# Loading attention and MoE operands as fp16 through GpSimd's software DMA queue, with VectorE pairing the heads

## Chip, cores and metric

The kernel runs on one core of one Trainium2 chip. The metric is the time of one execution in microseconds (us); several runs are made, and their median is compared. The engines are named as the profile names them: PE is TensorE's matmul, PEld its weight load, DVE is VectorE, ACT is ScalarE, POOL is GpSimd, and SP is the engine that issued every transfer so far. SPq and POOLq are their instruction queues.

## Reference, cut to what matters

An attention with an extra one in its denominator feeds a feed-forward layer that takes the largest of three products. The shapes are 8 batches, 12 heads, 448 positions and 64 values for each head, so 3584 tokens of 768 values; all four weights are 768 x 768. Every input and the output are fp32.

```python
scores = (q @ k.T) / sqrt(64)
m = max(scores, axis=-1)
e = exp(scores - m)
attn = e / (sum(e) + exp(-m) + 1e-09)
a = attn @ v                                  # [8, 12, 448, 64]
x = a.transpose(0, 2, 1, 3).reshape(3584, 768)
h = maximum(maximum(x @ w1, x @ w2), x @ w3)
out = h @ w_out
```

## Kernel before

**Tiles.** The work on q, k and v is cut into 24 groups: batch b and a third g of the heads, so four heads (GH) in each group. The 448 positions lie on 112 partitions with 4 positions (NCH) each. The function load_group (L78) brings q, k and v of one group as fp32 into tiles ld_q, ld_k and ld_v of [112, 4 heads, 4, 64], with three buffers for each name. One such transfer moves 448 runs of 1 KB, one for each partition and head. load_weight (L113) brings a weight in three parts of [128, 2, 768] fp32 into staging tiles wst, of which there are three buffers for all.

**Casts.** All operands of TensorE are fp16. POOL makes them. cast_qk (L133) writes q16 and k16 for each pair of heads, in the order [position, head, value] that the transposes want, in four instructions of 512 elements on each partition. cast_v (L148) multiplies v by LAMBDA = 256 in one instruction of 1024 elements. cast_weight (L124) copies each third of a weight from wst into w_sb.

**A group's work.** transpose_pair (L155) transposes k16 and q16 of a pair on PE into a PSUM tile trT (8 instructions, L161), and DVE copies that into qkT (L166). scores_visit (L169) makes two positions' worth of scores of a pair on PE (L178), and ACT takes the exponential into eT (L187). av_group (L196) makes the denominator with a matrix of ones and then the two halves of the numerator (L207); ACT makes the reciprocal as Exp(-Ln(den + 1)) in two steps (L218, L220), and DVE multiplies it in, into xT (L223). The factor 256 in v keeps the fp16 values large; it is divided out of the output at L265.

**The feed-forward pieces.** up_piece (L231) is six matmuls into one PSUM bank p_i (L237) and a DVE instruction that copies it (L245) or takes the maximum (L247). out_piece (L252) is six matmuls (L258), a DVE scaling (L265), and after every second one the stores from SP (L281). Pieces wait in a list, and moe (L298) takes them out by a credit of PE columns, so that each visit of the attention is followed by about as much feed-forward work. The PSUM pool ps1 has four banks, for trT, the three products of av_group, p_i and op_ps together.

**Order.** The schedule is written by hand: each engine runs its instructions in the order in which the program emits them, and waits where a tile isn't there. Before the loop, groups 0, 1 and 2 are requested, and groups 0 and 1 are cast. Iteration i of the loop (L324) first emits loads and casts for later groups, then four visits of group i. Visit 0 is followed by av_group of group i - 1, visits 1 and 2 by the two transpose_pair of group i + 1. The first pieces enter the list in iteration 3. The order of the loads on SP is q and k of group 0, q and k of group 1, v of both, group 2, w1, q and k of group 3, w2 of the reference's names, v of group 3, w3, group 4, w_out, group 5, and then one group in each iteration. (In the program's counting from 0 these weights are 0, 1, 2 and 3.) The stores of L281 are issued on SP too, so loads behind them wait for them.

Of the kernel before, what the change touches and what calls it, by code (L numbers as in the profile page):

```python
# [21 lines left out]
def kernel(  # L22
# [11 lines left out]
    nc = tc.nc  # L34

    B, H, S, D = q.shape
    NTOK, DM = out.shape
    DFF = moe_w1.shape[1]
    SC = 112
    NCH = S // SC  # L40
    NDC = DM // 128
    NFC = DFF // 128
    GH = 4
    NG = H // GH
    scale = 1.0 / math.sqrt(D)
# [5 lines left out]
            name=nc.get_next_instruction_name(),  # L51
# [4 lines left out]
    )  # L56

    cpool = ctx.enter_context(tc.tile_pool(name="const", bufs=1))
    ld_pool = ctx.enter_context(tc.tile_pool(name="ld", bufs=3))
    p16_pool = ctx.enter_context(tc.tile_pool(name="p16", bufs=4))  # L60
    v16_pool = ctx.enter_context(tc.tile_pool(name="v16", bufs=5))
    att_pool = ctx.enter_context(tc.tile_pool(name="att", bufs=4))
    wst_pool = ctx.enter_context(tc.tile_pool(name="wst", bufs=3))
    e_pool = ctx.enter_context(tc.tile_pool(name="e", bufs=2))
    small = ctx.enter_context(tc.tile_pool(name="small", bufs=2))
    xt_pool = ctx.enter_context(tc.tile_pool(name="xt", bufs=2))
# [9 lines left out]
    raw = {}  # L76

    def load_group(i, which="qkv", step=GH):  # L78
        b, g = groups[i]
        tiles = raw.setdefault(i, {})  # L80
        for name in which:
            tiles[name] = ld_pool.tile(
                [SC, GH, NCH, D], FP32, tag="ld_" + name, name="ld_" + name
            )
        for h0 in range(0, GH, step):
            for name in which:
                src = {"q": q, "k": k, "v": v}[name][b].rearrange(
                    "(g h) (p c) d -> g p h (c d)", g=NG, c=NCH
                )[g]
                nc.sync.dma_start(  # L90
                    out=tiles[name][:, h0 : h0 + step].rearrange("p h c d -> p h (c d)"),
                    in_=src[:, h0 : h0 + step],
                )

    load_group(0, "qk", 2)
    load_group(1, "qk")
    load_group(0, "v")
    load_group(1, "v")
    load_group(2)

    ident16 = cpool.tile([128, 128], MMDT, name="ident16")
    make_identity(nc, ident16)
    ones16 = cpool.tile([SC, 32], MMDT, name="ones16")
    nc.vector.memset(ones16, 1.0)
    one_b = cpool.tile([128, 1], FP32, name="one_b")
    nc.vector.memset(one_b, 1.0)

    w_sb = [cpool.tile([128, NDC, DFF], MMDT, name=f"w{i}") for i in range(4)]
    wout_sb = w_sb[3]

    wst_of = {}

    def load_weight(i):  # L113
        w = (moe_w1, moe_w2, moe_w3, moe_w_out)[i]
        for g in range(NG):
            wst = wst_pool.tile([128, 2, DFF], FP32, tag="wst", name="wst")
            wst_of[i, g] = wst
            if i < 3:
                src = w.rearrange("(g p hf) f -> g p hf f", g=NG, hf=2)[g]
            else:  # L120
                src = w.rearrange("(g hf p) f -> g p hf f", g=NG, hf=2)[g]
            nc.sync.dma_start(out=wst, in_=src)  # L122

    def cast_weight(i):  # L124
        for g in range(NG):
            nc.gpsimd.tensor_copy(  # L126
                out=w_sb[i][:, 2 * g : 2 * g + 2, :], in_=wst_of.pop((i, g))
            )


    state = {}

    def cast_qk(i):  # L133
        qf, kf = raw[i].pop("q"), raw[i].pop("k")
        qk16 = []
        for pr in range(GH // 2):
            q16 = p16_pool.tile([SC, NCH, 2, D], MMDT, tag=f"q16_{pr}", name=f"q16_{pr}")
            k16 = p16_pool.tile([SC, NCH, 2, D], MMDT, tag=f"k16_{pr}", name=f"k16_{pr}")
            nc.gpsimd.tensor_copy(  # L139
                out=q16, in_=qf[:, 2 * pr : 2 * pr + 2].rearrange("p h c d -> p c h d")  # L140
            )
            nc.gpsimd.tensor_copy(  # L142
                out=k16, in_=kf[:, 2 * pr : 2 * pr + 2].rearrange("p h c d -> p c h d")
            )
            qk16.append((q16, k16))
        state[i] = {"qk16": qk16, "qkT": []}

    def cast_v(i):  # L148
        v16 = v16_pool.tile([SC, GH, NCH, D], MMDT, tag="v16", name="v16")
        nc.gpsimd.tensor_scalar(  # L150
            out=v16, in0=raw[i].pop("v"), scalar1=LAMBDA, scalar2=None, op0=ALU.mult
        )
        state[i]["v16"] = v16

    def transpose_pair(i, pr):  # L155
        st = state[i]
# [39 lines left out]
    def av_group(i):  # L196
        b, g = groups[i]
        st = state.pop(i)
        eT, v16 = st["eT"], st["v16"]
        if g == 0:  # L200
            xT[b] = xt_pool.tile([128, NDC, S], MMDT, tag="xT", name="xT")

        def col_tiled(weights):
            bank = ps1.tile([128, 512], FP32, tag="bank1", name="av")
            for c in range(NCH):
                for hh in range(GH):
                    nc.tensor.matmul(  # L207
                        out=bank[32 * hh : 32 * hh + 32, 0:S],
                        lhsT=weights(hh, c),
                        rhs=eT[:, hh, c, :],  # L210
                        start=(c == 0),
                        stop=(c == NCH - 1),
                    )
# [6 lines left out]
        nc.scalar.activation(out=rb, in_=lnd, func=AF.Exp, scale=-1.0)  # L220
        for hf in range(2):
            num = col_tiled(lambda hh, c: v16[:, hh, c, hf::2])
            nc.vector.tensor_tensor(  # L223
                out=xT[b][:, 2 * g + hf, :], in0=num[:, 0:S], in1=rb, op=ALU.mult
            )
# [88 lines left out]
    visits = [(pr, cs) for pr in range(2) for cs in ((0, 1), (2, 3))]  # L314
    NI = len(groups)

    cast_qk(0)
    cast_qk(1)
    cast_v(0)
    cast_v(1)  # L320
    transpose_pair(0, 0)
    transpose_pair(0, 1)

    for i in range(NI):  # L324
        b, g = groups[i]
        if i == 0:
            cast_qk(2)
            cast_v(2)
            load_weight(0)
            cast_weight(0)  # L330
            load_group(3, "qk")
            cast_qk(3)
        elif i == 1:
            load_weight(1)
            cast_weight(1)
            load_group(3, "v")
            cast_v(3)
        elif i == 2:
            load_weight(2)
            cast_weight(2)  # L340
            load_group(4)
            cast_qk(4)
            cast_v(4)
            load_weight(3)
            cast_weight(3)
            load_group(5)
            cast_qk(5)
            cast_v(5)
        elif i + 3 < NI:
            load_group(i + 3)  # L350
            cast_qk(i + 3)
            cast_v(i + 3)
        for vi, (pr, cs) in enumerate(visits):
            scores_visit(i, pr, cs)
            if vi == 0:
                spare = gap - av_cols
                moe(spare / 2)
                if i > 0:
                    av_group(i - 1)
                moe(spare / 2)  # L360
                if i > 0 and g == 0:
                    add_pieces(b - 1)
            elif vi < 3:
                moe((gap - tr_cols) / 2)
# [38 lines left out]
```

## Time and profile before

| what | value |
|---|---|
| median of three runs (lowest, highest) | 393.98 us (389.93, 394.03) |
| the profiled execution's own time | 395.06 us |
| its span in the trace | 393.3 us |
| bytes read from HBM / written | 42.47 MB / 11.01 MB |
| POOL instructions | 138, busy 139.8 us |
| q, k, v transfers of 448 KB | 24 + 23 + 23, and 4 halves of 224 KB for group 0 |
| weight transfers of 768 KB | 9 + 3 |

A page of the profile has the engines' busy time, then the span in 40 slices (each digit is a busy share in tenths), the DMA queues, the chain of work that ended last, and the costliest groups of instructions. A row of a group gives line, engine, operation, out<-in with shapes and count, then total busy us and mean ns of one, then the idle time of the engine ahead of it and what ended it. The chain is followed back from the end: each step is what released the next one. Rows of the view by windows give, for a stretch of time, the busy us of each engine (with the number of its instructions), the clock granted to PE as a share of full speed, the mean busy share of the 16 DMA engines (it can exceed 1, since packets overlap) and GB/s. Rows of the timeline give start, length, engine, line and tiles.

### The profile page before, as it was taken

The numbers are of one execution on the slowest core, as the hardware profiler recorded it, in microseconds if no ns is written. First come the engines' busy times: TensorE is split into PE (matmuls) and PEld (weight loads), VectorE is DVE, ScalarE is ACT, GpSimd is POOL, SyncE is SP. The second block draws the span as 40 slices with busy tenths as digits, with TensorE's granted clock in tenths as the row PEclk, the third lists the DMA queues.
The fourth block names the chain that finished last, engine by engine and source line by source line (L and its number), as shares of the span: only waits on it lengthen the run. The fifth ranks groups of instructions, "written<-read, shape, count | busy, mean of one in ns | idle before, by whom it ended". The sixth has DMA issues, their size and how long they took to land.

```text
span 393.3 us, 7451 instructions
## 1 busy us (share of the span) xinstructions
PE 365.3 (93%) x3120; PEld 174.0 (44%) x3120; DVE 173.9 (44%) x298; ACT 192.8 (49%) x241; POOL 139.8 (36%) x138
## 2 busy tenths in 40 slices
PE   2886739999999999999999999999999999999995
PEld 1232314444444544445444544444444554445552
DVE  1122213543543644544544544544544554544553
ACT  1876405556555555555455564566364465462000
POOL 3876766990492007700572027500580000000000
PEclk9997758999999999999999999999999999999999
DMA  8999999954980289305980299205960320004005
GB/s 194 225 311 311 303 286 240 236 123 119 240 185 2 53 204 260 68 0 147 226 171 2 66 242 231 47 1 164 244 135 2 83 82 0 2 2 120 2 0 161
DMA packets 40067, 53.96 MB, mean 137 GB/s; under 512 B 2273, under 2 KB 34529, under 8 KB 40033
## 3 DMA queue, kind: packets, MB, share of 16 engines
q1 hardware_dynamic: 40032, 53.49, 56.5%
q8 instruction: 24, 0.39, 0.4%
q14 instruction: 11, 0.08, 0.1%
HBM read 42.47 MB, written 11.01 MB: 136 GB/s over the span
## 4 chain that ended last, share of the span: by engine, by line
PE 85%; DMA 9%; SPq 3%; POOL 1%; issue 0%; DVE 0%; POOLq 0%
PE p_i L237 43%; PE op_ps L258 14%; PE av L207 13%; PE stp L178 10%; DMA wst<-in_moe_w_dram 7%; PE trT L161 4%; DMA ld_k<-in_k_dram 3%; SPq L90 3%; SPq L122 1%; POOL w_127 L126 0%; POOL w_126 L126 0%; POOL k_0_400 L142 0%; DVE o_sb L265 0%; POOLq L142 0%
## 5 line engine op out<-in xcount | busy, mean ns | idle before, releaser
L187 ACT ACTIVATE eT<-stp 112x896 f16<-112x896 f32 x192 | 164.8, 915 | 161.7 <-PE stp L178 161.7
L247 DVE TENSOR_TENSOR hT<-hT,p_i 128x448 f16<-128x448 f16 x96 | 59.5, 620 | 57.8 <-PE p_i L237 57.8
L237 PE MATMUL p_i<-xT,w_126 128*128 128x448 f16 x288 | 65.0, 362 | 0.1
L237 PE MATMUL p_i<-xT,w_127 128*128 128x448 f16 x288 | 62.4, 353 | 0.0
L237 PE MATMUL p_i<-xT,w_128 128*128 128x448 f16 x288 | 62.2, 353 | 0.0
L178 PE MATMUL stp<-qkT 64*128 64x448 f16 x384 | 58.2, 375 | 4.2 <-ACT eT L187 3.9
L258 PE MATMUL op_ps<-w_129,hT 128*128 128x384 f16 x336 | 59.5, 326 | 0.0
L223 DVE TENSOR_TENSOR xT<-av,rb 128x448 f16<-128x448 f32 x48 | 27.9, 620 | 69.8 <-ACT rb L220 57.7
L265 DVE TENSOR_SCALAR o_sb<-op_ps 128x384 f32<-128x384 f32 x56 | 31.2, 557 | 28.9 <-PE op_ps L258 27.8
L245 DVE CAST hT<-p_i 128x448 f16<-128x448 f32 x48 | 29.9, 624 | 30.7 <-PE p_i L237 30.7
L258 PEld LDWEIGHTS <-hT 128*128 128x128 f16 x336 | 30.9, 98 | 24.8 <-issue 6.3
L166 DVE COPY qkT<-trT 128x896 f16<-128x896 f16 x48 | 29.6, 617 | 27.2 <-PE trT L161 27.2
L237 PEld LDWEIGHTS <-w_126 128*128 128x128 f16 x288 | 26.6, 100 | 29.2 <-issue 9.2
L237 PEld LDWEIGHTS <-w_127 128*128 128x128 f16 x288 | 25.9, 98 | 29.2 <-issue 8.9
L237 PEld LDWEIGHTS <-w_128 128*128 128x128 f16 x288 | 26.0, 98 | 28.7 <-issue 7.8
L178 PEld LDWEIGHTS <-qkT 64*128 64x128 f16 x384 | 12.0, 95 | 41.4 <-issue 41.1
L207 PE MATMUL av<-eT,ones_122 112*32 112x448 f16 x384 | 24.1, 373 | 0.0
L218 ACT ACTIVATE lnd<-av,one_b 128x448 f32<-128x448 f32 x24 | 15.3, 639 | 3.7 <-PE av L207 3.7
L220 ACT ACTIVATE rb<-lnd 128x448 f32<-128x448 f32 x24 | 13.8, 577 | 0.8
L207 PEld LDWEIGHTS <-ones_122 112*32 112x32 f16 x384 | 8.3, 98 | 13.2 <-issue 9.6
L139 POOL CAST q_0_1734<-ld_q 112x512 f16<-112x512 f32 x1 | 0.6, 609 | 25.0 <-PE trT L161 25.0
L139 POOL CAST q_0_2331<-ld_q 112x512 f16<-112x512 f32 x1 | 0.6, 610 | 24.7 <-DMA ld_q<-in_q_dram 24.7
(371 smaller groups left out, 273.3 us busy)
## 6 DMA issues: line engine op xcount, KB each, us to landing
ld_v<-in_v_dram SPq DMA_DIRECT2D x24, 448.0 KB, 11.7
ld_q<-in_q_dram SPq DMA_DIRECT2D x23, 448.0 KB, 9.7
ld_k<-in_k_dram SPq DMA_DIRECT2D x23, 448.0 KB, 11.3
wst<-in_moe_w_dram SPq DMA_DIRECT2D x9, 768.0 KB, 9.3
out_dram<-o_sb SPq DMA_DIRECT2D x8, 336.0 KB, 2.8
wst<-in_moe_w_out_dram SPq DMA_DIRECT2D x3, 768.0 KB, 11.9
out_dram<-o_sb SPq DMA_DIRECT2D x8, 288.0 KB, 2.7
out_dram<-o_sb SPq DMA_DIRECT2D x8, 240.0 KB, 2.8
```

Of the source, the lines that this page charges most:

```text
L161: nc.tensor.transpose(out=trT[:, n, ts(c, SC)], in_=t16[:, c, :, :], identity=ident16[0:SC, 0:SC],)
L166: nc.vector.tensor_copy(out=qkT, in_=trT.rearrange("p n s -> p (n s)"))
L178: nc.tensor.matmul(out=stp[:, hh, 0:S], lhsT=qkT[hh * D : hh * D + D, c * SC : c * SC + 128], rhs=qkT[hh * D : hh * D + D, S : 2 * S], sta ...
L187: nc.scalar.activation(out=st["eT"][:, 2 * pr : 2 * pr + 2, c, :], in_=stp[0:SC, :, 0:S], func=AF.Exp, scale=scale,)
L207: nc.tensor.matmul(out=bank[32 * hh : 32 * hh + 32, 0:S], lhsT=weights(hh, c), rhs=eT[:, hh, c, :], start=(c == 0), stop=(c == NCH - 1),)
L218: nc.scalar.activation(out=lnd, in_=den[:, 0:S], func=AF.Ln, bias=one_b)
L223: nc.vector.tensor_tensor(out=xT[b][:, 2 * g + hf, :], in0=num[:, 0:S], in1=rb, op=ALU.mult)
L237: nc.tensor.matmul(out=p_i[:, 0:S], lhsT=w_sb[i][:, dc, ts(fc, 128)], rhs=xT[b][:, dc, :], start=(dc == 0), stop=(dc == NDC - 1),)
L245: nc.vector.tensor_copy(out=dst, in_=p_i[:, 0:S])
L247: nc.vector.tensor_tensor(out=dst, in0=dst, in1=p_i[:, 0:S], op=ALU.max)
L258: nc.tensor.matmul(out=op_ps[:, 0:NW], lhsT=hT[bp][:, fc, ts(t, 128)], rhs=wout_sb[:, fc, ts(nh, NW)], start=(fc == 0), stop=(fc == NFC - 1),)
L265: nc.vector.tensor_scalar(out=o_sb[:, ts(nh, NW)], in0=op_ps[:, 0:NW], scalar1=1.0 / LAMBDA, scalar2=None, op0=ALU.mult,)
```

## The change

All loads move from SP to POOL's queue and land as fp16; there are no staging tiles and no POOL casts any more. The weights land straight in w_sb. The tiles ld_q, ld_k and ld_v are fp16 and have five buffers instead of three. av_group reads ld_v directly. The pairing of heads, which was part of the POOL cast, becomes pair_qk: four DVE copies fp16 to fp16 of 112 x 512 for each group, with two buffers; it is emitted behind visit 0 of iteration i for group i + 1. The factor 256 moves from v into the reciprocal, as a bias ln(256) of the second ACT step. The identity for the transposes is made by POOL behind the four requests of group 0 instead of behind all first requests. The stores stay on SP.

```diff
-    ld_pool = ctx.enter_context(tc.tile_pool(name="ld", bufs=3))
-    p16_pool = ctx.enter_context(tc.tile_pool(name="p16", bufs=4))
-    v16_pool = ctx.enter_context(tc.tile_pool(name="v16", bufs=5))
+    ld_pool = ctx.enter_context(tc.tile_pool(name="ld", bufs=5))
+    p16_pool = ctx.enter_context(tc.tile_pool(name="p16", bufs=2))
-    wst_pool = ctx.enter_context(tc.tile_pool(name="wst", bufs=3))
...
-                [SC, GH, NCH, D], FP32, tag="ld_" + name, name="ld_" + name
+                [SC, GH, NCH, D], MMDT, tag="ld_" + name, name="ld_" + name
...
-                nc.sync.dma_start(
+                nc.gpsimd.dma_start(
...
     load_group(0, "qk", 2)
+    ident16 = cpool.tile([128, 128], MMDT, name="ident16")
+    make_identity(nc, ident16)
     load_group(1, "qk")
...
-            wst = wst_pool.tile([128, 2, DFF], FP32, tag="wst", name="wst")
-            wst_of[i, g] = wst
...
-            nc.sync.dma_start(out=wst, in_=src)
+            nc.gpsimd.dma_start(out=w_sb[i][:, 2 * g : 2 * g + 2, :], in_=src)
...
-    def cast_qk(i):
+    def pair_qk(i):
...
-            nc.gpsimd.tensor_copy(
+            nc.vector.tensor_copy(
+                out=k16, in_=kf[:, 2 * pr : 2 * pr + 2].rearrange("p h c d -> p c h d")
+            )
+            nc.vector.tensor_copy(
                 out=q16, in_=qf[:, 2 * pr : 2 * pr + 2].rearrange("p h c d -> p c h d")
             )
...
-    def cast_v(i):
-        v16 = v16_pool.tile([SC, GH, NCH, D], MMDT, tag="v16", name="v16")
-        nc.gpsimd.tensor_scalar(
-            out=v16, in0=raw[i].pop("v"), scalar1=LAMBDA, scalar2=None, op0=ALU.mult
-        )
-        state[i]["v16"] = v16
...
-        eT, v16 = st["eT"], st["v16"]
+        eT, v16 = st["eT"], raw[i].pop("v")
...
-        nc.scalar.activation(out=rb, in_=lnd, func=AF.Exp, scale=-1.0)
+        nc.scalar.activation(out=rb, in_=lnd, func=AF.Exp, bias=ln_lam, scale=-1.0)
...
                 if i > 0 and g == 0:
                     add_pieces(b - 1)
+                if i + 1 < NI:
+                    pair_qk(i + 1)
```

The loop keeps its order of loads; the calls of cast_qk, cast_v and cast_weight are gone from it.

More of the change, by code (lines that the diff above doesn't have):

```diff
@@ L99 @@
     load_group(2)
-    ident16 = cpool.tile([128, 128], MMDT, name="ident16")
-    make_identity(nc, ident16)
     ones16 = cpool.tile([SC, 32], MMDT, name="ones16")
@@ L106 @@
     nc.vector.memset(one_b, 1.0)
+    ln_lam = cpool.tile([128, 1], FP32, name="ln_lam")
+    nc.vector.memset(ln_lam, math.log(LAMBDA))
     w_sb = [cpool.tile([128, NDC, DFF], MMDT, name=f"w{i}") for i in range(4)]
     wout_sb = w_sb[3]
-    wst_of = {}
     def load_weight(i):
@@ L121, in load_weight @@
                 src = w.rearrange("(g hf p) f -> g p hf f", g=NG, hf=2)[g]
[L122 to L127, printed above, removed]
-            )
+            nc.gpsimd.dma_start(out=w_sb[i][:, 2 * g : 2 * g + 2, :], in_=src)
     state = {}
-    def cast_qk(i):
+    def pair_qk(i):
         qf, kf = raw[i].pop("q"), raw[i].pop("k")
@@ L138, in cast_qk @@
             k16 = p16_pool.tile([SC, NCH, 2, D], MMDT, tag=f"k16_{pr}", name=f"k16_{pr}")
-            nc.gpsimd.tensor_copy(
+            nc.vector.tensor_copy(
+                out=k16, in_=kf[:, 2 * pr : 2 * pr + 2].rearrange("p h c d -> p c h d")
+            )
+            nc.vector.tensor_copy(
                 out=q16, in_=qf[:, 2 * pr : 2 * pr + 2].rearrange("p h c d -> p c h d")
-            )
-            nc.gpsimd.tensor_copy(
-                out=k16, in_=kf[:, 2 * pr : 2 * pr + 2].rearrange("p h c d -> p c h d")
             )
@@ L146, in cast_qk @@
         state[i] = {"qk16": qk16, "qkT": []}
-    def cast_v(i):
-        v16 = v16_pool.tile([SC, GH, NCH, D], MMDT, tag="v16", name="v16")
-        nc.gpsimd.tensor_scalar(
-            out=v16, in0=raw[i].pop("v"), scalar1=LAMBDA, scalar2=None, op0=ALU.mult
-        )
-        state[i]["v16"] = v16
     def transpose_pair(i, pr):
@@ L315 @@
     NI = len(groups)
[L317 to L320, printed above, removed]
+    pair_qk(0)
     transpose_pair(0, 0)
@@ L326 @@
         if i == 0:
-            cast_qk(2)
-            cast_v(2)
             load_weight(0)
-            cast_weight(0)
             load_group(3, "qk")
-            cast_qk(3)
         elif i == 1:
             load_weight(1)
-            cast_weight(1)
             load_group(3, "v")
-            cast_v(3)
         elif i == 2:
             load_weight(2)
-            cast_weight(2)
             load_group(4)
-            cast_qk(4)
-            cast_v(4)
             load_weight(3)
-            cast_weight(3)
             load_group(5)
-            cast_qk(5)
-            cast_v(5)
         elif i + 3 < NI:
             load_group(i + 3)
-            cast_qk(i + 3)
-            cast_v(i + 3)
         for vi, (pr, cs) in enumerate(visits):
```

## Prediction

> **What bounds the kernel now.** I read the page's slices first, then the chain of waits in order of time, then windows and the timeline around one group.
>
> ```profile
> span 393.3 us, 7451 instructions
> PE 365.3 (93%) x3120; PEld 174.0 (44%) x3120; DVE 173.9 (44%) x298; ACT 192.8 (49%) x241; POOL 139.8 (36%) x138
> PE   2886739999999999999999999999999999999995
> DMA  8999999954980289305980299205960320004005
> GB/s 194 225 311 311 303 286 240 236 123 119 240 185 2 53 204 260 68 0 147 226 171 2 66 242 231 47 1 164 244 135 2 83 82 0 2 2 120 2 0 161
> PE p_i L237 43%; PE op_ps L258 14%; PE av L207 13%; PE stp L178 10%; DMA wst<-in_moe_w_dram 7%; PE trT L161 4%; DMA ld_k<-in_k_dram 3%; SPq L90 3%; SPq L122 1%; POOL w_127 L126 0%; POOL w_126 L126 0%; POOL k_0_400 L142 0%; DVE o_sb L265 0%; POOLq L142 0%
> ```
>
> There are two stages. In the first six slices (a slice is 9.83 us) PE has gaps and the DMA engines are full; from the seventh slice to the end PE stands at 9 while DMA comes and goes. The chain says where the border lies.
>
> ```profile
> 13.29 16.55 DMA wst<-in_moe_w_dram
> 29.89 1.48 POOL w_126 L126
> 31.39 9.33 DMA wst<-in_moe_w_dram
> ...
> 40.77 1.48 POOL w_127 L126
> ...
> 43.12 11.27 DMA ld_k<-in_k_dram
> ...
> 54.50 0.62 POOL k_0_400 L142
> 55.17 0.93 PE trT L161 x8
> ...
> 212.72 2.38 PE av L207 x48
> ...
> 227.35 2.38 PE av L207 x48
> ```
>
> Until 54.39 (43.12 + 11.27) the end is set by loads, last by k of group 4, with three POOL casts between. From 55.17 on the chain is PE alone. So the change can win in the first 55 us only, and can lose in both stages. A group then takes 14.6 us (212.72 to 227.35).
>
> **The loads of the first stage.** Ahead of the end of k of group 4, both programs request, in the same order, 14 transfers' worth of q, k and v (groups 0 to 2 complete, q and k of group 3, v of group 3, q and k of group 4) and nine of weights.
>
> ```profile
> ld_k<-in_k_dram SPq DMA_DIRECT2D x23, 448.0 KB, 11.3
> wst<-in_moe_w_dram SPq DMA_DIRECT2D x9, 768.0 KB, 9.3
> 0.73 0.38 SPq L90 DMA_DIRECT2D ld_q<-in_q_dram  x1
> 3.76 0.61 POOL L139 CAST q_0_130<-ld_q 112x512 f16<-112x512 f32 x1 [2.46 <-DMA ld_q<-in_q_dram]
> 10.00:15.00 5.00, 3.73 (x26) 1.72 (x23) 0.62 (x1) 4.16 (x6) 3.18 (x5) 1.00 1.14 221
> 20.00:25.00 5.00, 4.42 (x48) 1.54 (x40) 1.87 (x3) 2.75 (x5) 4.38 (x5) 1.00 1.02 357
> 70.00:75.00 5.00, 5.00 (x36) 2.22 (x34) 3.46 (x6) 2.21 (x4) 4.59 (x5) 1.00 1.13 237
> ```
>
> That is 14 x 458,752 B = 6.42 MB and 9 x 786,432 B = 7.08 MB, 13.50 MB. In 70 to 75 us only q, k and v move: 237 GB/s, so 1.94 us for each. In 20 to 25 mostly a weight moves: 357 GB/s, so 2.20 us for each. One after the other they take 14 x 1.94 + 9 x 2.20 = 46.9 us. The first half transfer was requested at 0.73 and in use at 3.76; less its own 0.97 us (229,376 B at 237 GB/s) that is a delay of 2.06. So k of group 4 could be there at 0.73 + 2.06 + 46.9 = 49.7, against 54.39.
>
> What the change takes away here is what held SP back: the three staging buffers of the weights, freed by POOL's casts (the two rows of 1.48 us in the chain). POOL now only has requests, and runs ahead through all five buffers. Bounds: at best 4.7 us are won (54.39 - 49.7). At worst nothing, since the DMA line of the page shows these engines at 9 in the second to eighth slice: they never stood idle for lack of requests. Up to 54.39 the GB/s line gives (194 + 225 + 311 + 311 + 303) x 9.83 + 286 x 5.2 = 14.7 MB, 1.2 MB more than lay ahead of k, so later transfers shared the engines; deeper queues would not undo that. I take 1.5 us won, nearer to the DMA line than to the sum of packet rates.
>
> The price of a POOL request is not in the trace, where POOL requests nothing. Nearest rows:
>
> ```profile
> 43.12 0.48 SPq L90 DMA_DIRECT2D ld_k<-in_k_dram  x1
> L150 POOL TENSOR_SCALAR v_146<-ld_v 112x1024 f16<-112x1024 f32 x1 | 2.8, 2772 | 0.3 <-DMA ld_v<-in_v_dram 0.3
> ```
>
> SP takes 0.48 us where it isn't held; the longest POOL instruction takes 2.77. I let 0.48 to 2.77 stand as bounds and expect about 1.1 (their geometric mean), below the 1.94 and 2.20 that a transfer lasts, so requests hide behind transfers. The first is not hidden: up to 2.3 us later, contained in the 1.5 above.
>
> That fp32 read and fp16 written go at the plain rate is also assumed, not shown. Bounds: 221 GB/s, the lowest full stretch above, for all bytes; and, upward, 357 for q, k and v too. I take today's rates, since the bytes read are the same.
>
> **The POOL casts** (139.8 us) vanish from an engine that is off the chain after 55 us: worth nothing there. The V scale goes with them, and the second ACT step gets a bias: no instruction is added.
>
> **The DVE copies.** Four for each group, 96 in all, fp16 from SBUF to SBUF, 112 x 512; no such row exists. DVE rows:
>
> ```profile
> L265 DVE TENSOR_SCALAR o_sb<-op_ps 128x384 f32<-128x384 f32 x56 | 31.2, 557 | 28.9 <-PE op_ps L258 27.8
> L245 DVE CAST hT<-p_i 128x448 f16<-128x448 f32 x48 | 29.9, 624 | 30.7 <-PE p_i L237 30.7
> L166 DVE COPY qkT<-trT 128x896 f16<-128x896 f16 x48 | 29.6, 617 | 27.2 <-PE trT L161 27.2
> 200.00:275.00 75.00, 75.00 (x673) 35.90 (x666) 37.08 (x64) 41.90 (x54) 23.13 (x21) 1.00 0.47 110
> ```
>
> From 384 to 448 elements, 67 ns are added: 1.05 ns an element, with 155 ns fixed. The fp16 copy of 896 costs (617 - 155) / 896 = 0.52 an element. So a copy of 512 costs 155 + 264 = 419 ns by the fp16 row, and 691 if it goes at one element per 1.05 ns. I take 419, the same operation and type: 40 us in all, 1.68 for a group. DVE's 37.08 of 75 us becomes about 46: no bound. Where the run of four falls matters:
>
> ```profile
> 212.65 0.94 PE L207 MATMUL av<-eT,ones_122 112*32 112x448 f16 x16
> 215.03 1.31 PE L237 MATMUL p_i<-xT,w_127 128*128 128x448 f16 x6
> 215.46 1.16 DVE L223 TENSOR_TENSOR xT<-av,rb 128x448 f16<-128x448 f32 x2 [2.56 <-ACT rb L220]
> 216.53 0.61 DVE L247 TENSOR_TENSOR hT<-hT,p_i 128x448 f16<-128x448 f16 x1
> 217.90 0.36 PE L161 MATMUL trT<-ident_117,k_0_2332 112*128 112x112 f16 x4
> 218.10 0.36 PE L161 MATMUL trT<-ident_117,q_0_2331 112*128 112x112 f16 x4
> 218.11 0.62 DVE L247 TENSOR_TENSOR hT<-hT,p_i 128x448 f16<-128x448 f16 x1 [0.97 <-PE p_i L237]
> ```
>
> They come behind the DVE instruction at 216.53, so from 217.14: k16 is there at 217.56, q16 at 217.98. PE transposes k at 217.90 and q at 218.10: just in time, no cost. At 691 ns q16 comes at 218.52, 0.4 us late in each of the 19 groups behind the first stage: +8. Queued behind the copies is the emptying of p_i at 218.11, now 218.82; three more banks of ps1 cover 0.7 us. Without that cover PE would lose it in each group, 13 us. I take 0. If a load came late, pair_qk's wait would hold these evictions too, and PE behind them; in the first stage PE stands at the same transposes anyway, and later the loads of a group (1.38 MB, 5.8 us at 237 GB/s) have 14.6 us and run several groups ahead.
>
> **Sum.** 395.06 (span 393.3 and 1.76 around it) - 1.5 + 0 = 393.6 for a profiled execution. That one was 1.1 above the median of its kernel, 393.98; on the median the forecast is 392.5.
>
> **Rivals.**
> Faster loads: writing half the bytes shortens the short transfers, and q, k and v go at 357 GB/s, 1.29 us each. Then 14 x 0.65 = 9.1 us more are won, 383.4. For it: their 237 GB/s at a full DMA shows that these 1 KB runs are limited by something else than the weights are. Against it: the 1 KB reads stay. The Trainium skill (DMA: Bandwidth & Descriptors, Where 436 GB/s comes from) has a load bound on the HBM side at about 358 GB/s; the row of 357 agrees, and by that rule the weights gain nothing from shorter writes.
>
> Slower loads: a cast in flight, or requests that POOL makes slowly, stretch the first stage. At 221 GB/s for all, k of group 4 comes at 2.79 + 1 (a later first request) + 13.50 / 0.221 = 64.9, 10.5 later: 404.5. At 2.77 us for each of 25 requests (four are halves), 69.3 + 2.8 = 72.1, 17.7 later: 411.7. It decides from a request of 2 us, or a rate under about 250 GB/s over the stage. For it: PE had nothing else to do before 55.17, so each microsecond counts. Against it: nothing in the trace but the size of the transfers.
>
> Copies and requests exclude each other: if a DVE copy between SBUF tiles and a POOL request can't run together, the copies come late in every group. The place is bad: POOL's next three requests are freed by the end of av_group's last product, at 215.03 above, because v of five groups earlier goes free there, and the copies want DVE at 217.14. With 1.1 us a request, two end at 217.23, k16 at 217.65, the third at 218.75, q16 at 219.17 instead of 218.10 at the latest: 1.1 us late. This happens in some 15 groups (loads of groups 9 to 23): +17, 411. With 0.48 us a request they end at 216.5, and it costs nothing; it decides from (217.14 - 215.03) / 3 = 0.7 us on; at 2.77, 3.3 x 15 = +50. This case is slower where I forecast no change. The Trainium skill (SBUF — State Buffer, Who interferes with whom) states such an exclusion between a GpSimd request's descriptor writing and two-port VectorE copies; no run here shows it, as no DVE instruction before copies from SBUF to SBUF.
>
> **Chances.** No change to speak of, as summed: 0.38, with its own range 388 to 397. Faster loads 0.22. Slower loads 0.24. Exclusion 0.16. About 1% is what a measurement of this kernel tells from no change (389.93 to 394.03 before). Faster by over 1% (under 390.0): all of faster loads and 0.08 of the first, 0.30. Within 1%: 0.27 of the first and 0.07 of mild forms of the slower two, 0.34. Slower: 0.36. The range reaches from 382, past the faster loads, to 424, which holds both slower prices and leaves out their far ends.
>
> **What would show it.** Right: the first p_i behind the long gap starts near 54, the windows of 10 to 50 us keep 220 to 360 GB/s, no wait of trT on DVE beyond 0.2 us after 60 us, PE at 9 from the seventh slice on, DVE near 214 us busy. Copies near 0.42 us. Faster loads: over 280 GB/s where only q, k and v move. Slower loads: the gap ends after 60, POOL requests back to back or DMA below full. Exclusion: copies that last over 1 us or start late behind a POOL request, and groups of over 15 us. My forecast is wrong if the restart of PE moves by more than 5 us or a group's 14.6 us grows.

## The result, and the profile after

The changed kernel takes 379.41 us (median of three runs, 379.26 to 380.31) against 393.98: a ratio of 0.966 with a 95% interval of 0.958 to 0.974. The forecast of 392.5 missed it, and so did its range, by 2.6 us. The profiled execution took 379.41 us, 15.65 less than the one before.

The page of the changed kernel, with the lines that answer to those of before:

```profile
span 377.6 us, 7320 instructions
PE 358.3 (95%) x3120; PEld 172.0 (46%) x3120; DVE 194.7 (52%) x395; ACT 194.5 (52%) x241; POOL 59.4 (16%) x92
PE   2777999999999999999999999999999999999995
DMA  7999998555508625455236555077010410013005
GB/s 92 185 208 206 204 196 121 73 136 68 73 2 151 111 54 75 60 139 75 32 43 89 126 101 73 6 128 141 2 26 0 128 43 0 2 32 95 2 0 168
q0 software_dynamic: 35552, 21.24, 40.8%
HBM read 42.47 MB, written 11.01 MB: 142 GB/s over the span
```

PE now stands at 9 from the fifth slice on (a slice is 9.44 us), not from the seventh. The GB/s line needs care: the queue that casts (q0) moved 21.24 MB by the page while the program read 42.47 MB. For a load that casts, the rows count what is written, half of what is read. So 206 there is 412 GB/s read.

The chain of the changed kernel around the border of the two stages (start, length, what):

```profile
29.02 12.52 DMA ld_k<-in_k_dram
...
41.63 0.30 DVE k_0_563 L129
...
41.98 0.57 PE trT L144 x8
42.55 1.14 PE p_i L220 x6
```

k of group 4 lands at 41.54 (54.39 before), and PE starts its transposes at 41.98 (55.17 before): 13.2 us earlier. From there to the end of the span it is 335.6 us, against 338.1. So 13.2 of the 15.65 us come out of the first stage, and 2.5 out of what follows. The six p_i matmuls behind these transposes took 2.24 us before and take 1.14 now. The windows of the kernel before say why (the column ahead of the DMA share is the granted clock):

```profile
50.00:55.00 5.00, 0.00 (x0) 0.00 (x0) 0.00 (x0) 0.00 (x0) 2.58 (x3) 0.58 1.11 236
55.00:60.00 5.00, 4.83 (x21) 2.04 (x22) 1.25 (x2) 1.12 (x2) 4.76 (x5) 0.50 1.04 356
60.00:65.00 5.00, 5.00 (x32) 2.32 (x31) 2.13 (x4) 2.32 (x3) 3.25 (x3) 0.90 1.13 227
```

PE had waited there, and came back to a clock of 0.50. In the changed kernel it waits 0.32 us for k of group 4, and its clock stays at 1.00 (the first stage thus ends with loads and with PE's own work at nearly the same time):

```profile
15.00:20.00 5.00, 4.30 (x36) 1.38 (x37) 0.54 (x1) 4.34 (x6) 2.00 (x4) 1.00 1.20 211
40.00:45.00 5.00, 4.68 (x32) 2.20 (x31) 3.05 (x9) 1.84 (x4) 2.34 (x4) 1.00 1.17 206
50.00:55.00 5.00, 5.00 (x66) 2.12 (x64) 1.82 (x4) 2.92 (x4) 2.98 (x5) 1.00 1.45 196
110.00:185.00 75.00, 74.88 (x686) 36.18 (x679) 40.69 (x82) 42.07 (x53) 10.46 (x15) 1.00 0.49 84
```

In 50 to 55 us only q, k and v move: 196 GB/s written, 392 read, so 1.17 us for each transfer of 458,752 B (1.94 before). In 15 to 20 us, where mostly a weight moves, it is 211 written, 422 read: 1.86 us for 786,432 B (2.20 before). In the steady stretch PE is as full as before.

The copies that are new on DVE, around the end of group 14, in rows of the timeline:

```profile
215.68 0.71 POOL L88 DMA_DIRECT2D ld_k<-in_k_dram  x1
215.93 0.58 DVE L129 COPY k_1_2917<-ld_k 112x512 f16<-112x512 f16 x1
216.50 0.36 PE L144 MATMUL trT<-ident_97,k_0_2913 112*128 112x112 f16 x4
```

A request takes POOL 0.71 us. This copy lasts 0.58 and ends just behind the request; the median copy lasts 0.283. Of the 96 copies 15 last 445 to 582 ns, each begun within a request and ended about 0.1 us behind its end; 24 others also begin within a request and are not lengthened. From group 5 on all are done when PE comes for them.

### The profile page after: what moved, and what is told of

It is laid out like the page before. It is cut to its first block, busy times and chain, and to the rows that moved or that the text cites. A ratio compares the mean times of both kernels' runs of the same rounds, so it can differ in the third digit from the quotient of the medians.

```text
span 377.6 us, 7320 instructions
## 1 busy us (share of the span) xinstructions
PE 358.3 (95%) x3120; PEld 172.0 (46%) x3120; DVE 194.7 (52%) x395; ACT 194.5 (52%) x241; POOL 59.4 (16%) x92
## 3 DMA queue, kind: packets, MB, share of 16 engines
q0 software_dynamic: 35552, 21.24, 40.8%
HBM read 42.47 MB, written 11.01 MB: 142 GB/s over the span
## 4 chain that ended last, share of the span: by engine, by line
PE 84%; DMA 9%; ACT 2%; POOL 2%; DVE 1%; issue 1%; DVEq 0%; POOLq 0%
PE p_i L220 43%; PE op_ps L241 15%; PE av L190 11%; PE stp L161 10%; PE trT L144 4%; DMA w_123<-in_moe_w_dram 3%; DMA ld_k<-in_k_dram 3%; DMA ld_q<-in_q_dram 2%; DVE xT L206 1%; ACT eT L170 1%; ACT rb L203 1%; ACT lnd L201 1%; POOL ld_q L88 1%; POOL ld_k L88 1%; POOL ld_v L88 0%
## 5 line engine op out<-in xcount | busy, mean ns | idle before, releaser
L220 PE MATMUL p_i<-xT,w_122 128*128 128x448 f16 x288 | 63.0, 353 | 0.4
L220 PE MATMUL p_i<-xT,w_123 128*128 128x448 f16 x288 | 62.4, 353 | 0.0
L220 PE MATMUL p_i<-xT,w_124 128*128 128x448 f16 x288 | 62.2, 353 | 0.0
L161 PE MATMUL stp<-qkT 64*128 64x448 f16 x384 | 56.3, 364 | 4.9 <-ACT eT L170 4.8
L88 POOL DMA_DIRECT2D ld_v<-in_v_dram x24 | 16.8, 702 | 192.3 <-PE av L190 126.3
L190 PE MATMUL av<-eT,ld_v 112*32 112x448 f16 x768 | 41.8, 361 | 0.0
L190 PEld LDWEIGHTS <-ld_v 112*32 112x32 f16 x768 | 21.0, 99 | 16.8 <-issue 1.7
L190 PE MATMUL av<-eT,ones_116 112*32 112x448 f16 x384 | 23.3, 364 | 0.0
L88 POOL DMA_DIRECT2D ld_q<-in_q_dram x25 | 17.7, 709 | 6.9 <-DMA w_124<-in_moe_w_dram 1.5
L88 POOL DMA_DIRECT2D ld_k<-in_k_dram x25 | 17.6, 703 | 4.4 <-DMA w_123<-in_moe_w_dram 1.1
```

The source lines that it names most:

```text
L88: nc.gpsimd.dma_start(out=tiles[name][:, h0 : h0 + step].rearrange("p h c d -> p h (c d)"), in_=src[:, h0 : h0 + step],)
L161: nc.tensor.matmul(out=stp[:, hh, 0:S], lhsT=qkT[hh * D : hh * D + D, c * SC : c * SC + 128], rhs=qkT[hh * D : hh * D + D, S : 2 * S], sta ...
L190: nc.tensor.matmul(out=bank[32 * hh : 32 * hh + 32, 0:S], lhsT=weights(hh, c), rhs=eT[:, hh, c, :], start=(c == 0), stop=(c == NCH - 1),)
L220: nc.tensor.matmul(out=p_i[:, 0:S], lhsT=w_sb[i][:, dc, ts(fc, 128)], rhs=xT[b][:, dc, :], start=(dc == 0), stop=(dc == NDC - 1),)
```

## Experiments

Two questions: what made the loads of the first stage faster, and whether the copies or the requests cost anything.

### The loads by themselves

Five kernels hold only the loads of eight groups and of the four weights, in plain order; `eng` and `T` differ, and the tiles have a buffer each unless said otherwise.

```python
for i in range(8):
    for name, t in (("q", q), ("k", k), ("v", v)):
        tl = pool.tile([SC, GH, NCH, D], T)
        eng.dma_start(out=tl, in_=src)       # 448 runs of 1 KB
for i, w in enumerate(weights):
    for g in range(NG):
        last = pool.tile([128, 2, DFF], T)
        eng.dma_start(out=last, in_=src)
```

**Plain fp32 on SP.** 

> Loads alone: 24 transfers of q, k and v, then the 12 thirds of the weights, each into a tile of its own, plain fp32 from SP; attention and feed-forward are left out and zeros are stored at the end. Both theories: the rates of the kernel before, about 237 GB/s while only q, k and v move and about 350 while weights move; 24 x 1.94 + 12 x 2.20 = 73 us of loading.

**Plain fp32 on POOL.** 

> The same loads, plain fp32, requested by POOL; attention and feed-forward are left out. Theory (the shorter writes of the cast make the loads faster, not the queue): as from SP, about 237 and 350 GB/s, 73 us. Rival (POOL's queue itself is faster, whatever is written): about 390 and 410 GB/s, 24 x 1.17 + 12 x 1.91 = 51 us.

**fp16 on POOL.** 

> The same loads, cast to fp16 on the way, requested by POOL; attention and feed-forward are left out. Both theories: the rates of the changed kernel, 196 GB/s written (392 read) while q, k and v move and 205 written (410 read) while weights move; 51 us of loading.

Windows of the three, in this order (the engine columns are DVE, ACT and POOL, since PE has nothing to do); the first row of each has only q, k and v in it, the second only weights:

```profile
20.00:25.00 5.00, 0.00 (x0) 0.00 (x0) 0.00 (x0) 1.00 1.12 260
50.00:55.00 5.00, 0.00 (x0) 0.00 (x0) 0.00 (x0) 1.00 1.02 418
```

```profile
20.00:25.00 5.00, 0.00 (x0) 0.00 (x0) 1.96 (x4) 1.00 1.04 269
50.00:55.00 5.00, 0.00 (x0) 0.00 (x0) 1.75 (x3) 1.00 1.01 417
```

```profile
20.00:25.00 5.00, 0.00 (x0) 0.00 (x0) 2.97 (x5) 1.00 1.45 195
40.00:45.00 5.00, 0.00 (x0) 0.00 (x0) 0.70 (x1) 1.00 1.08 211
```

The times are 101.16, 102.22 and 87.7 us. The queue alone makes no difference (260 and 269, 418 and 417; over the windows from 10 to 45 us 260 to 266 and 246 to 269 for q, k and v). Landing as fp16 lifts q, k and v from about 265 to 390 GB/s read (195 written) and leaves the weights at about 420 (211 written). So the cast speeds the transfers of 1 KB runs and not those of the weights. And the loads of the kernel before were slower than the same loads alone: its 237 and 357 GB/s stand against 260 and 418.

**Plain fp32 on SP, with POOL copying a scratch tile all the time.** 

> The loads alone, plain fp32 from SP, as in the first run of them (262 GB/s while only q, k and v move, 419 while weights move), with POOL copying a scratch tile fp32 to fp16, 45 times 1.47 us, beside them; attention and feed-forward are left out. Theory (the POOL casts of the kernel before slow its loads): 237 GB/s and about 357, as there. Rival (something else held the loads of before): 262 and 419.

102.18 us, with 252 to 280 GB/s for q, k and v and 410 to 418 for the weights: POOL's copies do not slow these transfers. That theory fell.

**Plain fp32 on SP, with three buffers for each name,** freed by a tiny DVE copy as soon as a transfer has landed. 

> The loads alone, plain fp32 from SP, but with three buffers for each of q, k, v and the weights' staging, each freed by a copy of four columns on DVE as soon as it has landed; attention and feed-forward are left out. Theory (too few transfers outstanding slow the loads of before): 237 GB/s while q, k and v move, and under 400 while weights move. Rival (the POOL casts, or anything else): 262 and 419.

```profile
50.00:55.00 5.00, 0.34 (x2) 0.00 (x0) 0.00 (x0) 1.00 1.00 339
60.00:65.00 5.00, 0.34 (x2) 0.00 (x0) 0.00 (x0) 1.00 0.92 325
```

102.55 us. q, k and v keep 262 to 284, but the weights fall from 418 to between 325 and 397. The DMA share still reads 1.00 at 339 GB/s, as it read 1.02 at 418.

### Undoing one part of the change

**q, k and v plain again.** Requests stay on POOL, the weights still land as fp16; three buffers, and DVE makes the casts, v's too.

```diff
-    ld_pool = ctx.enter_context(tc.tile_pool(name="ld", bufs=5))
+    ld_pool = ctx.enter_context(tc.tile_pool(name="ld", bufs=3))
...
-                [SC, GH, NCH, D], MMDT, tag="ld_" + name, name="ld_" + name
+                [SC, GH, NCH, D], FP32, tag="ld_" + name, name="ld_" + name
...
+    def cast_v(i):
+        v16 = v16_pool.tile([SC, GH, NCH, D], MMDT, tag="v16", name="v16")
+        nc.vector.tensor_copy(out=v16, in_=raw[i].pop("v"))
```

> The changed kernel, but q, k and v arrive as plain fp32 on POOL's queue (three buffers) and DVE casts them: in the pairing copies, and v in one more copy for each group; the weights still cast on the way. Theory (shorter writes): each of the 14 transfers of q, k and v ahead of k of group 4 takes 1.94 us again instead of 1.17, so the first product of the feed-forward behind the transposes of group 4 moves from 42.4 by about 10.8 to 53, PE idles for about 10 us and runs at a lower clock behind it, and the time is 379.4 + 10.8 + 2 = about 392. Rival (the queue): 379 to 381.

```profile
32.53 14.38 DMA ld_k<-in_k_dram
...
47.49 0.93 PE trT L150 x8
48.42 2.24 PE p_i L226 x6
```

387.97 us (386.62 to 390.32), ratio to the kernel before 0.984 [0.980, 0.989]. k of group 4 lands at 46.91, 5.4 us later than in the changed kernel, PE waits 3.42 us for it, and the time is 8.5 longer, more than half of the gain. Not all of that is the rate of the loads: in the profile (the slowest of the four runs, 390.32 us) PE restarts 5.5 us later, and from there to the end it takes 341.0 us instead of 335.6. The lower clock, three buffers and DVE's casts can all act there; they were not told apart. The landing moved half as far as expected, the time about two thirds.

**The weights plain again.** w1 to w3 land as fp32 in staging tiles, POOL casts them; q, k, v and w_out still land as fp16. Once with eight staging tiles, once with three, so that a POOL cast stands ahead of six of the nine requests.

```diff
-            nc.gpsimd.dma_start(out=w_sb[i][:, 2 * g : 2 * g + 2, :], in_=src)
+            if (i, g) in before_req:            # three tiles: weight i - 1, same g
+                cast_third(*before_req[i, g])
+            wst = wst_pool.tile([128, 2, DFF], FP32, tag="wst", name="wst")
+            nc.gpsimd.dma_start(out=wst, in_=src)
```

> The changed kernel, but w1, w2 and w3 land as plain fp32 in eight staging tiles and POOL casts them (nine casts of about 1.5 us); q, k, v and w_out still land as fp16. Theory (casting speeds only the 1 KB runs; the weights of the kernel before were slow because they had only three staging tiles and waited for casts): the weights keep about 420 GB/s, so k of group 4 lands at 41 to 43 us and the time is 379 to 381. Rival (landing as fp16 speeds the weights too when the kernel's other work runs): 9 transfers of 2.20 instead of 1.87 us, so k of group 4 lands at 44 to 47 and the time is 383 to 386.

> As the last, but with three staging tiles, so that each weight's request stands behind a POOL cast of the weight before it, as the kernel before had it behind SP's queue. Theory (three staging tiles hold the weights back): the weights fall to 325 to 397 GB/s as with three tiles in the loads alone, 2.0 to 2.4 us each, and requests of q, k, v behind them come late too: k of group 4 lands at 44 to 49 and the time is 382 to 388. Rival (the number of staging tiles is without effect, as six instead of three in the kernel before gained nothing measurable): the same as with eight tiles, within 1 us.

**The changed kernel again, beside them.** 

> The changed kernel itself on the same chip as the last two, for comparison: 379 to 380.5 us, k of group 4 landed at 41 to 42 us.

The changed kernel took 379.51 us (378.64 to 379.66), and k of group 4 landed at 40.97. With eight tiles: 387.2 (384.95 to 387.87). With three: 383.74 (381.45 to 385.39). The fewer tiles were the faster kernel, against both theories, and the timeline of the one with eight tiles shows why:

```profile
25.00:30.00 5.00, 4.12 (x42) 1.63 (x43) 0.00 (x0) 4.31 (x6) 4.70 (x5) 0.66 1.04 418
```

```profile
31.42 0.90 DVE L150 COPY k<-ld_k 112x512 f16<-112x512 f16 x1
32.24 3.38 DVE L153 COPY q<-ld_q 112x512 f16<-112x512 f16 x1
32.58 7.18 POOL L131 CAST w<-wst 128x1536 f16<-128x1536 f32 x5
35.53 4.37 DVE L150 COPY k<-ld_k 112x512 f16<-112x512 f16 x1
39.97 0.46 PE L165 MATMUL trT<-ident,k 112*128 112x112 f16 x3 [2.88 <-DVE k L150]
```

The loads did what the theory of the loads said: plain fp32 weights read 418 GB/s, and k of group 4, requested at 31.15, landed at 41.81, within 1 us of the changed kernel. So the cast by itself does next to nothing for the weights. But three copies of group 3, beside POOL's row of casts, lasted 0.90, 3.38 and 4.37 us instead of 0.28, together 7.8 us too long, and two of them stand in the chain that ended last; the kernel is 7.7 us slower. PE comes to the transposes of group 4 only at 50.51, long after k. With three tiles, where POOL asked for each later weight only behind a cast, k of group 4 was requested at 36.69 and landed at 43.4, 2.4 us later than in the changed kernel. That is not what the 4.2 us of this version are, though, as its chain shows:

```profile
5.26 7.17 DMA ld_k<-in_k_dram
...
23.14 1.04 DVE k L150
...
33.83 1.48 DVE q L153
...
46.66 0.40 PE trT L165 x8
```

Behind the load that ended at 12.43 no load stands in the chain up to there. PE came to the transposes of group 4 at 46.49, 3.1 us after k had landed, and did not wait for it. It was late from its own work, 4.5 us later than in the changed kernel; the two copies of the chain, 1.03 and 1.56 us long, are among the causes, and a lower clock in 25 to 45 us (0.57 to 0.89). So later requests put the landing back, and their price in time is not shown.

**Both plain again,** with three staging tiles: the load pattern of the kernel before without SP's queue. 

> The changed kernel with every load that stands ahead of k of group 4 as plain fp32: q, k, v with three buffers and cast by DVE, w1 to w3 through three staging tiles and cast by POOL, all requested on POOL. It is the kernel before's pattern of loads without SP's queue and without POOL's casts of q, k and v. Theory (the two parts add: 5.4 us for the cast of q, k, v and 1.9 us for three staging tiles): k of group 4 lands at 48 to 50 us. Rival (the pattern itself makes the rest, whatever the queue): it lands at 53 to 55, as in the kernel before.

```profile
40.88 0.71 POOL ld_q L90
41.59 9.27 DMA ld_k<-in_k_dram
...
50.95 0.44 DVE k L151
...
51.43 0.98 PE trT L171 x8
52.41 2.24 PE p_i L247 x6
```

393.38 us, ratio to the kernel before 0.999 [0.996, 1.003]: the whole gain is gone. k of group 4 lands at 50.86, between the two expectations and nearer the theory's. In time the parts nearly add, 8.5 for q, k, v and 4.2 for the weights against 13.9 for both, but by luck, since the 4.2 were no wait for loads. In the landing they don't: 5.4 and 2.4 make 7.8, both together 9.3 (50.86 against 41.54).

**Six staging tiles in the kernel before** (wst 3 to 6; p16 4 to 2 and v16 5 to 4, to make room). 

> The kernel before with six staging buffers for the weights instead of three (and, for the room, two buffers instead of four for q16 and k16 and four instead of five for v16). Theory (a full DMA line hides that three staging buffers, freed by POOL in its order, hold the weights at about 310 GB/s instead of 420): w2 no longer waits for POOL's casts of w1, the weights ahead of k of group 4 take about 5 us less, the transposes of group 4 start near 50 instead of 55, and the time is about 388. Rival (the DMA line means what it says, and staging costs nothing): 393 to 394.

k of group 4 is requested at 33.68 instead of 43.12, but lands only 2.8 us earlier, at 51.58. The ratio is 0.997 [0.992, 1.002] over ten runs (389.93 to 399.48), no gain that can be measured. More staging tiles alone don't mend the kernel before. Nor do they speed its weights: the steps from one landing to the next, added up over the nine weight transfers, make 21.4 us here, 21.7 in the kernel before and 17.9 in the changed one.

### Delaying the loads, and the clock

**w_out ahead of group 4 in the changed kernel.**

```diff
             load_weight(2)
-            load_group(4)
             load_weight(3)
+            load_group(4)
```

> The changed kernel with the three thirds of w_out requested ahead of group 4 instead of behind it. Theory (the first stage ends with the landing of k of group 4, which follows the bytes ahead of it): 3 x 1.9 = 5.6 us later, at 47.2 instead of 41.5; PE idles for about 5.7 us ahead of the transposes of group 4, and runs at a lower clock behind that, which costs 2 more: 379.4 + 5.6 + 2 = 387. Rival (PE waits there for 0.3 us only, so the work ahead of it, not the loads, sets the end): within 1 us of 379.4, because the next thing that is late only moves into the gap.

```profile
33.22 13.26 DMA ld_k<-in_k_dram
...
46.92 0.93 PE trT L144 x8
47.85 2.24 PE p_i L220 x6
```

```profile
45.00:50.00 5.00, 3.08 (x14) 1.49 (x14) 2.50 (x7) 0.00 (x0) 2.90 (x5) 0.50 1.45 196
```

385.39 us (385.25 to 386.39), ratio to the kernel before 0.980 [0.978, 0.982]. A landing 5 us later costs 6.0: each microsecond that the landing is later counts, and PE, which waits 4.65 us for k, comes back to a clock of 0.50.

**The same with 20 idle matmuls in the gap,** ahead of the second visit's transposes in iteration 3. 

> The changed kernel with w_out ahead of group 4, as before in this study (385.4), and 20 matmuls of 128 x 448 whose result nobody reads put into PE's gap ahead of the transposes of group 4. Theory (of the 6.0 us that w_out ahead of group 4 cost, about 1 was the lower clock behind the gap): the granted clock from 45 to 55 us is 1.0 instead of 0.5 to 0.9, and the time is about 384.3. Rival (the clock is not worth anything in the end): 385.4 or more.

The clock stays at 1.00, the p_i matmuls behind the gap last 1.29 us, and the time is 384.76 (384.17 to 385.47), 0.6 less. The ratios to the kernel before, 0.980 [0.978, 0.982] and 0.978 [0.973, 0.982], overlap.

**36 such matmuls in the kernel before.** 

> The kernel before, with 36 matmuls of 128 x 448 whose result nobody reads put ahead of the transposes of group 4, into the gap of 7.9 us in which PE waits there. Theory (part of what the change won, 2.5 us behind the restart, is that PE's clock no longer falls after a long wait): the granted clock from 50 to 65 us is 1.0 instead of 0.5 to 0.9, and the time falls by about 2.5 us, to 391.5 beside 394. Rival (the 2.5 us come from the faster loads or the missing POOL casts in the second stage): no change, or up to 1 us longer.

From the restart to the end it was 335.3 us instead of 338.1 in the profile, but over ten runs the ratio is 1.000 [0.997, 1.003]. Inconclusive: the 2.5 us are seen in profiles and not in the times.

### The copies and the requests

**Requests head by head from group 9 on,** twelve for a group instead of three.

```diff
-            load_group(i + 3)
+            load_group(i + 3, step=1 if i >= 6 else GH)
```

> The changed kernel with the loads of groups 9 to 23 requested head by head, 12 requests for a group instead of 3, so that POOL requests for about 8 us in each group and not 2.1. Theory (a pairing copy that starts inside a POOL request waits for its end, and only the short requests of 0.70 us keep that off the path): nearly every copy lasts 0.4 to 0.9 us instead of 0.28, k16 and q16 come up to 1 us late for the transposes in these 15 groups, and the time is 383 to 392. Rival (no exclusion; the few long copies of the changed kernel are chance): copies of 0.28, 379 to 380.

```profile
L129 DVE COPY k<-ld_k 112x512 f16<-112x512 f16 x48 | 13.6, 284 | 8.4 <-DMA ld_k<-in_k_dram 8.4
```

380.4 us (378.64 to 381.72), as the changed kernel. 71 of the 96 copies begin within a request, two of them are lengthened (459 and 385 ns), and k's mean is 284 ns. That a request stops every copy beside it, as I had it in the rival, fell; what is left is the 15 copies of the changed kernel, held up by at most 0.3 us.

**POOL arithmetic beside the copies.**

```diff
             load_group(i + 3)
+            if i >= 6:
+                for _ in range(6):
+                    nc.gpsimd.tensor_copy(out=scr16, in_=scr32)
```

> The changed kernel with six POOL copies of a scratch tile (128 x 1536, fp32 to fp16, 1.48 us each) behind the three requests of each group from 9 on; no part of the reference is touched. Theory (POOL's arithmetic, unlike its requests, stops VectorE's copies between SBUF tiles, as the 3.38 and 4.37 us copies beside POOL's casts suggest): copies that begin beside them last until a run of POOL copies ends, up to 9 us, and PE waits for them: 2 to 6 us in each of 18 groups, 415 to 490. Rival (those two copies were late for another reason): copies stay at 0.28 us and the time at 379 to 381.

```profile
220.50 6.37 POOL L325 CAST scr<-scr 128x1536 f16<-128x1536 f32 x4
221.00 1.14 DVE L133 COPY k<-ld_k 112x512 f16<-112x512 f16 x1
222.05 0.28 DVE L136 COPY q<-ld_q 112x512 f16<-112x512 f16 x1
222.26 1.55 DVE L133 COPY k<-ld_k 112x512 f16<-112x512 f16 x1
```

385.97 us (384.97 to 386.24), 6.5 more than the changed kernel on another chip. It holds for 15 groups (iterations 6 to 20; the expectation counted 18), so 0.43 us for a group. POOL's arithmetic does stop the copies (k's mean is 842 ns), but here one POOL copy at a time, not the whole run of them. The Trainium skill (SBUF — State Buffer, Who interferes with whom) has it that the two engines share a pair of ports, and that when VectorE works in a two-port mode whoever issues first holds the pair for the whole instruction and the other blocks. These copies agree with it, at up to 1.55 us beside POOL copies of some 1.5; the 3.38 and 4.37 us of above outlast one POOL cast of 1.48, so there a copy waited for more than one. The copies beside requests, 15 of 39 lengthened in the changed kernel and 2 of 71 in the experiment before this one, mostly do not.

**q and k of group 0 by SP as plain fp32** (cast by DVE), so that the first transposes come earlier. 

> The changed kernel, but q and k of group 0 come plain from SP as fp32 and DVE's pairing copies cast them, so that POOL's first request is already for group 1. Theory (the first 42 us follow the loads, and in the first 5 us the DMA engines wait for requests): the first transposes at 4.6 instead of 5.4 us, k of group 4 about 2 us earlier, 378.0, a gain of 1 to 2 us. Rival (from 9 us on ACT and PE set the pace of groups 0 to 3, and PE waits for k of group 4 only 0.3 us): 379.0 to 379.4, no change.

```profile
2.17 6.95 DMA first_k<-in_k_dram
...
9.62 0.93 PE trT L148 x8
```

381.87 us (one of the six runs took 1257.79), ratio to the kernel before 0.970 [0.965, 0.974], some 2.5 slower than the changed kernel. The first pair came at 4.98 instead of 5.40, but the second at 9.62 instead of 7.69: its k took 6.95 us to land, while POOL had requested eight other transfers. None of these versions beats the changed kernel.

## Why the prediction was wrong

**The step that failed** is the rates: "I take today's rates, since the bytes read are the same". A transfer of q, k or v took 1.17 us instead of 1.94, a weight 1.86 instead of 2.20. With these exchanged, the prediction's own sum gives the change: the 23 transfers take 14 x 1.17 + 9 x 1.86 = 33.1 us instead of 46.9, 13.8 less; the first request goes out at 1.29 instead of 0.73, 0.6 more; 54.39 - 13.8 + 0.6 = 41.2, and k of group 4 landed at 41.54.

It works as a difference only. Added up from the first request the sum is some 5 us short in both kernels (49.7 against 54.39, and 1.29 + 2.06 + 33.1 = 36.5 against 41.54), because these rates are those of the windows chosen and not the mean. The landings give the mean: from the second landing to that of k of group 4, the steps that end with q, k or v add up to 28.04 us before and 18.66 after, those that end with a weight to 21.66 and 17.92. So 9.4 us come from q, k and v and 3.7 from the weights.

Why q, k and v got faster is shown: it is the halved writes (plain and casting loads alone on one queue, 265 and 390 GB/s read). Undone in the kernel, with three buffers, that puts the landing back by 5.4 us, less than the 9.4. Why the weights got faster is open. It is not the cast by itself (417 plain and 422 cast alone, 418 plain with eight tiles). That staging tiles hold requests back is at most a part: by themselves the loads of weights fall to between 325 and 397 GB/s with three tiles, and three tiles in the changed kernel put the landing back by 2.4 us; but six tiles instead of three in the kernel before left the weights as slow as they were. With both undone the landing goes back by 9.3 of the 12.8 us between the two kernels.

**"At worst nothing, since the DMA line shows these engines at 9."** This reading failed with it. A share of 1.14 stood at 221 GB/s, 1.00 at 339, 1.02 at 418. So in these traces a full DMA line does not say that the engines move what they could.

**Faster loads,** the rival at 0.22, had the right mechanism and too small a price. Its 1.29 us for q, k and v came from a ceiling of 357 GB/s that is none, and it left the weights at 2.20. The rule of the Trainium skill (DMA: Bandwidth & Descriptors, Where 436 GB/s comes from) that was weighed against it, a bound of about 358 GB/s on the HBM side, is not borne out: 417 to 420 GB/s were read here, by the only core that ran. The same page (Measured) has 425 GB/s for transfers of 16 MB on one core alone, which these windows come near. The 2.5 us behind the restart it did not have either.

**The clock** was in no term: the prediction looked at when PE comes back, not at how. In the profile it is 2.5 us; in the times it was not shown (0.6 us with overlapping intervals, and nothing over ten runs).

**What bounds the kernel** was right for the kernel before: loads up to k of group 4, then PE. In the changed kernel the two meet: PE waits 0.32 us for k of group 4, and in the profile beside the staging experiments not at all (k landed at 40.97, the transposes began at 42.04). Loads that are faster still would win next to nothing there. The steady groups did not change. **The copies** were right in cover and in cost, nothing; a copy is 0.283 us, not 0.419, so DVE is busy 194.7 us, not 214. **The request** is 0.70 us against the 1.1 taken, and hides as said. That is just the point from which the exclusion rival was to decide, and it didn't: the mechanism itself does not show for most copies beside requests. It exists beside POOL's arithmetic, of which the changed kernel has none left, the identity apart. That POOL lost its casts was thus not "worth nothing", as the prediction has it: with casts left on POOL, the copies that the change puts on DVE cost 7.7 us in one experiment and are among the causes of 4.2 in another. Nor did POOL run ahead through all five buffers, as the prediction also says: between 10 and 40 us each of its requests waited 0.4 to 2.4 us until an earlier transfer had landed, those of weights too, whose tiles nothing else uses.

**Open.** The landing in the kernel before, 54.39, is 3.5 us later than with the same pattern on POOL's queue, though the times are the same; what SP's queue or POOL's casts of q, k and v do there was not tried by itself. Nor is it known why plain q, k and v read 237 GB/s in the kernel before and 260 alone. Why 15 copies beside requests were lengthened and 24 not is open too; the trace shows a pattern: the 15 began 0.35 to 0.46 us before the request's end, and of the 24 all but one began earlier or later than that.

## What to carry to other kernels

Where a stage is bound by loads, measure the rate that the transfers reach alone, by size of run and type at the destination, and don't carry over the rate that the kernel happens to show under a full DMA line. A cast in the load pays where runs are short (1 KB here). What it frees besides, staging tiles and the requests that wait for them, has to be tried and not assumed: here six staging tiles instead of three gained nothing that can be measured. Before paying for faster loads, see how long PE really waits for them. When copies move to VectorE, look at what POOL computes at that moment, not at its requests.

## What the runs showed of the hardware

- A load from fp32 to fp16 of 1 KB runs reads 390 GB/s, plain loads alone 246 to 284; with 6 KB on each partition both read about 420.
- The profile counts a casting load by the bytes written.
- A request on POOL takes 0.70 us for 448 runs and 0.55 for most thirds of a weight, and between 10 and 40 us POOL's further ones waited until an earlier transfer had landed (0.4 to 2.4 us each); whether the chip or the program's semaphores made them wait is open.
- A VectorE copy between SBUF tiles of 0.28 us lasts up to 1.55 beside POOL copies of a scratch tile, and 3.38 and 4.37 beside POOL's weight casts.
- After a wait of 4.65 us PE came back to a clock of 0.50, after one of 0.32 us to 1.00.
